# Loading expert 0's second weight in two halves around a value load, with later landings in the schedule

## The chip, the cores and the metric

One core of one Trainium2 chip at a time. The metric is the device time of one execution in microseconds (us). Every kernel gave the reference's result.

## The reference, cut to what matters

Block-sparse attention over 4 batches of 8 heads (768 positions, 64 wide) makes a matrix x of 3072 rows and 512 columns. A mixture of 8 experts follows, with gates from Sinkhorn iterations, so every expert sees every row:

```python
logits = x @ w_gate
P = np.exp(logits - logits.max())
for _ in range(8):
    P /= P.sum(1, keepdims=True) + 1e-09
    P /= P.sum(0, keepdims=True) + 1e-09
    P *= N / E
for e in range(E):                      # E = 8
    h = np.maximum(x @ w1[e], 0.0)      # w1[e]: 512 x 1024
    out += P[:, e:e + 1] * (h @ w2[e])  # w2[e]: 1024 x 512
```

Expert 0 needs no gate until its end, so the kernel runs it beside the attention. Its second weight, w2, is the load that the change is about.

## The kernel before

The kernel describes its work as units, each with an engine, an estimated cost and the units it depends on. A planner puts the units of each engine in order from these estimates alone, and then the program is written in that order. At run time each engine goes through its list in order and waits by semaphores. So an estimate never makes a wait wrong, but it decides what stands ahead of the wait.

```python
def load_w2(e):
    w2s[e] = wpool.tile([128, KF, DM], F16, tag="w2", name="w2")
    nc.gpsimd.dma_start(out=w2s[e][:], in_=moe_w2[e].rearrange("(fk p) d -> p fk d", p=128))

# A load as the planner sees it: issue on POOL, time on the DMA queue,
# and 0.9 us until the data counts as landed.
def load(key, fn, issue, us, deps=()):
    last[0] = add("POOL", issue, fn, [last[0], *deps])
    last[1] = add("DMA", us, None, [add("RING", 0, None, [last[0]], lag=1.4 if last[1] else 0.9), last[1]], 100.0)
    U[key] = add("LAND", 0, None, [last[1]], lag=0.9)

# The projection of expert 0, in two parts: hidden chunks 0-3, then 4-7.
p0 = add("PE", 0.88, lambda c=c: project0(key, c, 0), evac[0:4] + [U["w2"]], pr + 0.1 + c * 0.02, opens=[buf])
p1 = add("PE", 0.88, lambda c=c: project0(key, c, 1), evac[4:8] + [p0], pr + 0.11 + c * 0.02, uses=[buf])

# The order of the loads (cut): the first batch, w1 in four parts, then
load_pair(PB, "kqv")                     # k, q, v of the second batch's first pair of heads
load("w2", lambda: load_w2(0), 0.85, 4.0)
# ... then constants (memsets on POOL) and the later pairs
```

All these loads cast f32 to a 16-bit type and go through one queue, issued by POOL. "Pair" below is a pair of heads; PB = 4 pairs make a batch.

The softmax here doesn't subtract the row's maximum and nothing guards it: scores larger than these inputs give would overflow.

## Time and profile before

| | before |
|---|---|
| median of the first 3 runs | 668.64 us (668.12 to 669.35) |
| profiled span | 666.7 us |
| TensorE (PE) busy | 657.9 us, 99% |
| idle of PE before the first projection with w2 | 1.34 us |

POOL's own timeline (start, length, engine, line, operation, output from input): it shows when the two loads of the argument were issued.

```profile
23.24 1.04 POOL L287 DMA_DIRECT2D vx<-in_v_dram  x1
24.24 0.91 POOL L196 DMA_DIRECT2D w<-in_moe_w_dram  x1
```

An issue is busy for about 1 us, but that is not the landing. In the same trace's list of DMA issues this w2 landed 10.5 us after its issue began, at 34.7.

### The profile page before, as it was taken

The page shows a single profiled execution, that of the slowest core. Times are in us where ns is not written, and L with a number is a line of the kernel's source. Part 1 is how long each engine was busy: PE and PEld are TensorE (multiplying, and loading weights), DVE is VectorE, ACT ScalarE, POOL GpSimd, SP SyncE. Part 2 cuts the span into 40 slices and gives each one's busy share as a digit, 9 for nine tenths or more (in the row PEclk, how much of TensorE's full clock was granted, in tenths as well). Part 3 has the DMA queues.
Part 4 walks back from the last instruction along what each step waited for, and adds up shares of the span by engine and source line. Part 5 has one row for each costly group of instructions (what it writes and reads, how often), then busy time and mean ns, then how long its engine had stood idle before and what let it go on. Part 6 is the DMA issues. An engine that isn't in the chain of part 4 may idle for free.

```text
span 666.7 us, 13260 instructions
## 1 busy us (share of the span) xinstructions
PE 657.9 (99%) x5132; PEld 434.0 (65%) x5132; DVE 549.2 (82%) x1035; ACT 410.5 (62%) x768; POOL 198.3 (30%) x256
## 2 busy tenths in 40 slices
PE   8999999999999999999999999999999999999996
PEld 4656665555676666666666666666666666666665
DVE  7889978799989787888789887888778877988776
ACT  6767766555986566556565665656665656556652
POOL 8899622100132222222221222222122213222123
PEclk9999999999999999999999999999999999999999
DMA  9999992700863647473654656373837465334656
GB/s 168 165 149 145 132 88 43 127 0 1 137 112 64 117 75 116 79 127 64 98 102 76 123 83 106 65 127 61 130 64 130 77 95 95 64 64 112 159 134 198
DMA packets 112542, 67.89 MB, mean 102 GB/s; under 512 B 77920, under 2 KB 90464, under 8 KB 112480
## 3 DMA queue, kind: packets, MB, share of 16 engines
q0 software_dynamic: 94800, 57.46, 65.7%
q1 hardware_dynamic: 17152, 9.58, 6.5%
q8 instruction: 40, 0.66, 0.4%
q14 instruction: 22, 0.18, 0.1%
q10 hardware_dynamic: 528, 0.02, 0.0%
HBM read 52.45 MB, written 6.29 MB: 88 GB/s over the span
## 4 chain that ended last, share of the span: by engine, by line
PE 94%; DMA 3%; POOL 2%; issue 0%; DVE 0%; ACT 0%; POOLq 0%; DVEq 0%
PE yps L813 22%; PE pA L762 22%; PE pY L813 17%; PE pQ L762 11%; PE yps L214 6%; PE hps L209 6%; PE pR L762 5%; DMA w<-in_moe_w_dram 3%; PE sg L345 1%; PE tkq L301 1%; PE av L433 1%; PE vs L355 1%; PE av L439 1%; POOL vx L287 1%; PE tx L548 1%; PE ss L459 1%
## 5 line engine op out<-in xcount | busy, mean ns | idle before, releaser
L813 PEld LDWEIGHTS <-h 128*128 128x128 f16 x2352 | 230.1, 98 | 89.3 <-issue 1.0
L841 POOL DMA_DIRECT2D out_acc<-y x120 | 101.5, 880 | 372.0 <-ACT y L837 97.8
L837 ACT ACTIVATE y<-pY,P_sb 128x256 f32<-128x256 f32 x168 | 79.8, 476 | 124.2 <-PE pY L813 122.5
L828 DVE SCALAR_TENSOR_TENSOR out_acc<-yps,P_sb,out_acc 128x512 f32<-128x512 f32 x128 | 95.2, 744 | 30.2 <-PE yps L813 30.0
L796 DVE TENSOR_TENSOR h<-h 128x1024 f16<-128x1024 f16 x168 | 109.0, 684 | 1.2
L813 PE MATMUL pY<-w,h 128*128 128x256 f16 x672 | 100.2, 273 | 0.6 <-ACT y L837 0.6
L762 PE MATMUL pA<-xT,w 128*128 128x512 f16 x336 | 98.5, 379 | 0.0
L813 PE MATMUL yps<-w2sum,h 128*128 128x256 f16 x672 | 98.1, 273 | 0.0
L813 PE MATMUL yps<-w,h 128*128 128x256 f16 x672 | 93.3, 273 | 0.0
L828 DVE SCALAR_TENSOR_TENSOR out_acc<-pY,P_sb,out_acc 128x512 f32<-128x512 f32 x84 | 62.9, 748 | 29.9 <-PE pY L813 28.2
L762 PEld LDWEIGHTS <-w 128*128 128x128 f16 x672 | 65.8, 98 | 30.9 <-issue 0.2
L762 PEld LDWEIGHTS <-w1sum 128*128 128x128 f16 x504 | 49.3, 98 | 44.2
L784 DVE CUSTOM_DVE_ANT_0 h<-pQ,snap 128x512 f16<-128x512 f32 x84 | 57.6, 685 | 6.0 <-ACT snap L205 3.3
L784 DVE CUSTOM_DVE_ANT_0 h<-pA,snap 128x512 f16<-128x512 f32 x84 | 57.3, 683 | 6.0 <-PE pA L762 5.9
L200 ACT ACTIVATE h<-pA 128x512 f16<-128x512 f32 x84 | 50.6, 603 | 12.4 <-PE pA L762 12.2
L200 ACT ACTIVATE h<-pR 128x512 f16<-128x512 f32 x84 | 50.1, 596 | 7.5 <-PE pR L762 7.4
L205 ACT COPY pR<-pA 128x512 f32<-128x512 f32 x84 | 48.0, 571 | 7.4 <-PE pA L762 6.4
L813 PE MATMUL pY<-w2sum,h 128*128 128x256 f16 x336 | 50.4, 273 | 0.0
L762 PE MATMUL pA<-xsum,w 128*128 128x512 f16 x168 | 50.0, 379 | 0.0
L762 PE MATMUL pQ<-xsum,w1sum 128*128 128x512 f16 x168 | 50.0, 379 | 0.0
L762 PE MATMUL pQ<-xT,w1sum 128*128 128x512 f16 x168 | 50.0, 379 | 0.0
L762 PE MATMUL pA<-xsum,w1sum 128*128 128x512 f16 x168 | 50.0, 379 | 0.0
(149 smaller groups left out, 845.9 us busy)
## 6 DMA issues: line engine op xcount, KB each, us to landing
out_acc<-y POOLq DMA_DIRECT2D x120, 256.0 KB, 3.4
w<-in_moe_w_dram POOLq DMA_DIRECT2D x15, 1024.0 KB, 10.6
out_dram<-out_acc SPq DMA_DIRECT2D x24, 256.0 KB, 2.5
qst<-in_q_dram POOLq DMA_DIRECT2D x32, 96.0 KB, 5.8
vx<-in_v_dram POOLq DMA_DIRECT2D x15, 192.0 KB, 6.6
kst<-in_k_dram POOLq DMA_DIRECT2D x24, 96.0 KB, 6.0
w<-in_moe_w_dram POOLq DMA_DIRECT2D x4, 256.0 KB, 7.9
kst<-in_k_dram POOLq DMA_DIRECT2D x3, 192.0 KB, 4.7
```

The lines of the kernel that those rows point to most:

```text
L200: nc.scalar.activation(out=out, in_=in_, func=AF.Relu, bias=0.0, scale=1.0)
L205: (nc.scalar.copy if eng == "ACT" else nc.vector.tensor_copy)(out=out, in_=in_)
L209: nc.tensor.matmul(hp[:, 0:n], lhsT=w1s[e][:, dk, f * 128:(f + 1) * 128], rhs=xT[:, dk, t0:t0 + n], start=(dk == 0), stop=(dk == KD - 1))
L214: nc.tensor.matmul(yp[:, d], lhsT=h[:, f, c * 128:(c + 1) * 128], rhs=w2s[e][:, f, d], start=(f == 0), stop=(f == KF - 1))
L287: nc.gpsimd.dma_start(out=v_x[i % NQ][:].rearrange("p j g x -> p (j g) x")[:, :, 0:D], in_=v[b, h0:h0 + 2].rearrange("j (g p) d -> p (j g) ...
L762: nc.tensor.matmul(dst[:], lhsT=lhsT, rhs=rhs, start=first and k == 0, stop=k == HK - 1, skip_group_check=True)
L784: nc.vector._custom_dve(dve_ops.TENSOR_ADD_SAT, out=ring(e, p, q)[:, q % 2, blk, :], in0=at[src, e, p, q][:], in1=at.pop(("snap", n, e, p, ...
L796: nc.vector.tensor_tensor(out=h[:, :, out_, :], in0=h[:, :, a, :], in1=h[:, :, b, :], op=op)
L813: nc.tensor.matmul(dst[:, d], lhsT=lhsT, rhs=rhs, start=f == 0 and n in (1, 5, 2), stop=f == HF - 1, skip_group_check=True)
L828: nc.vector.scalar_tensor_tensor(out=o, in0=y, scalar=scalar, in1=o, op0=ALU.mult, op1=ALU.add)
L837: nc.scalar.activation(out=at[key][:, d], in_=src, func=AF.Copy, bias=0.0, scale=P_sb[:, t, e:e + 1])
L841: nc.gpsimd.dma_start(out=o, in_=at.pop(("y", e, p, c, key))[:], accum_op=ALU.add)
```

## The change

The intent is to have the projection's first part wait for half of w2 only, to let that half come ahead of v, and to tell the planner that later loads land later, so that it puts more work ahead of their first use. Cut to its core:

```diff
-    def load_w2(e):
+    def load_w2(e, part=0, parts=1):
...
+        fk = slice(part * KF // parts, (part + 1) * KF // parts)
+        nc.gpsimd.dma_start(out=w2s[e][:, fk, :], in_=moe_w2[e].rearrange("(fk p) d -> p fk d", p=128)[:, fk, :])
...
-        def load(key, fn, issue, us, deps=()):
+        def load(key, fn, issue, us, deps=(), lag=0.9):
...
-            U[key] = add("LAND", 0, None, [last[1]], lag=0.9)
+            U[key] = add("LAND", 0, None, [last[1]], lag=lag)
...          # v of later batches: lag 2.3; their k and q: lag 1.8; first batch: 0.9 as before
-                p0 = add("PE", 0.88, lambda c=c: project0(key, c, 0), evac[0:4] + [U["w2"]],
+                p0 = add("PE", 0.88, lambda c=c: project0(key, c, 0), evac[0:4] + [w2_0[0]],
...
-                p1 = add("PE", 0.88, lambda c=c: project0(key, c, 1), evac[4:8] + [p0],
+                p1 = add("PE", 0.88, lambda c=c: project0(key, c, 1), evac[4:8] + [p0, w2_0[1]],
...
-        load_pair(PB, "kqv")
-        load("w2", lambda: load_w2(0), 0.85, 4.0)
+        load_pair(PB, "kq")
+        load(("w2", 0), lambda: load_w2(0, 0, 2), 0.85, 2.0, (), 2.3)
+        load_pair(PB, "v")
+        load(("w2", 1), lambda: load_w2(0, 1, 2), 0.85, 2.0, (), 2.3)
```

More of the change, by code (lines that the diff above doesn't have):

```diff
@@ L192, in load_w1 @@
             in_=moe_w1[e].rearrange("(dk p) f -> p dk f", p=128)[:, :, part * fw:(part + 1) * fw])
-    def load_w2(e):
-        w2s[e] = wpool.tile([128, KF, DM], F16, tag="w2", name="w2")
-        nc.gpsimd.dma_start(out=w2s[e][:], in_=moe_w2[e].rearrange("(fk p) d -> p fk d", p=128))
+    def load_w2(e, part=0, parts=1):
+        if part == 0:
+            w2s[e] = wpool.tile([128, KF, DM], F16, tag="w2", name="w2")
+        fk = slice(part * KF // parts, (part + 1) * KF // parts)
+        nc.gpsimd.dma_start(out=w2s[e][:, fk, :], in_=moe_w2[e].rearrange("(fk p) d -> p fk d", p=128)[:, fk, :])
     def relu(eng, out, in_):
@@ L869, in load_pair @@
                     load(("v", i), lambda: load_v(i), 1.05, 1.85 if i < PB else 1.6,
-                         [U.get(("A", old, 1)), U.get(("near", old))])
+                         [U.get(("A", old, 1)), U.get(("near", old))], 0.9 if i < PB else 2.3)
                 elif i < PB and c in "qr":
@@ L876, in load_pair @@
                     load((c, i), lambda z=z: load_qk(i, z), 0.75 if i < PB else 1.65,
-                         1.2 if i < PB else 1.4, [U.get(("tr", old, z)), U.get(("tr", old, 2))])
+                         1.2 if i < PB else 1.4, [U.get(("tr", old, z)), U.get(("tr", old, 2))], 0.9 if i < PB else 1.8)
         def pair_start(i, prio):
@@ L991, in expert0 @@
             pr = 1000.0 + n
-            w = [U["w1", n] for n in range(4)]
+            w, w2_0 = [U["w1", n] for n in range(4)], [U["w2", n] for n in range(2)]
             evac, old = [], [U.get(("pj", halves[n - 2], c)) for c in range(HG)] if n >= 2 else []
```

## The prediction

> **What bounds the kernel now.** I read the page's busy lines first, then the PE line of the 40 slices, then the chain of waits, and last the timeline of PE and of POOL around the one DMA piece that stands in that chain late. The page:
>
> ```profile
> PE 657.9 (99%) x5132; PEld 434.0 (65%) x5132; DVE 549.2 (82%) x1035; ACT 410.5 (62%) x768; POOL 198.3 (30%) x256
> PE   8999999999999999999999999999999999999996
> PEclk9999999999999999999999999999999999999999
> ```
>
> TensorE is busy 657.9 of 666.7 us, at the full granted clock in every slice. So only what shortens PE's stream of matmuls, or fills a hole in it, can shorten the kernel: 666.7 - 657.9 = 8.8 us of holes are all there is. The chain of waits says where one of them comes from (start, length, what):
>
> ```profile
> 8.48 2.03 POOL vx L287 x2
> 10.51 0.67 POOL w L190
> 11.18 9.34 DMA w<-in_moe_w_dram
> 20.52 0.28 issue
> 20.81 0.82 POOL kst L282
> 21.63 1.64 POOL qst L282 x2
> 23.27 0.97 POOL vx L287
> 24.24 10.49 DMA w<-in_moe_w_dram
> 34.73 0.04 issue
> 34.77 1.02 PE yps L214 x4
> ```
>
> The last DMA piece is expert 0's w2: issued at 24.24, landed at 34.73. From 34.77 on the chain is PE alone. The timeline of PE at that place:
>
> ```profile
> 31.52 0.81 PE L209 MATMUL hps<-xT,w 128*128 128x384 f16 x4
> 32.26 0.38 PE L345 MATMUL sg<-qT,kT 64*128 64x160 bf16 x6
> 32.58 0.51 PE L548 MATMUL tx<-ident_x,xs 128*128 128x128 f16 x6
> 32.92 0.51 PE L355 MATMUL vs<-vx,m_blk 128*128 128x128 bf16 x6
> 34.77 1.02 PE L214 MATMUL yps<-w,h 128*128 128x512 f16 x4 [1.34 <-DMA w<-in_moe_w_dram]
> ```
>
> PE stands still for 1.34 us until w2 is there. It is the only such hole after the start. The others, from the same timeline: 1.27 before the first matmul, 0.47 + 0.26 + 0.17 for the first q, the first v and a part of w1, before the change has any effect. The stretch 600 to 667 us has 61.59 busy of 67.00, so about 5.1 us lie at the end (66.7 - 61.59): the last results leaving. The rows from 35 to 600 show full slices (100.00 busy in each 100 us). 1.27 + 0.47 + 0.26 + 0.17 + 1.34 + 5.1 = 8.6 of the 8.8.
>
> **What the Trainium skill says.** (1) "Perfetto Trace Analysis", Identifying the Most-Contended Engine: matmul busy share is not a good measure of the distance to roofline, weight-load busy is a better one. Here 99% against 65%, so PE is not at its peak; but this change makes no matmul cheaper, and for a hole in an in-order stream the idle column is what counts. (2) Same page, DMA Instruction - SWDGE: the profiler's end of a GpSimd DMA is the end of descriptor generation, not of the movement. The trace agrees: w2's instruction took 0.91 us, its data landed 10.49 us after it began. So a second half costs POOL about 0.9 us more, and says nothing yet of landing. (3) "DMA: Bandwidth & Descriptors", SWDGE vs HWDGE vs iDMA: only GpSimd DMAs can cast. The weights are cast from f32 to f16, which fits their all being on POOL's queue; there the order of issue decides. (4) Same page, Anatomy of one DMA: about 2.0 us + bytes / 436 GB/s, so 4.4 us for w2's 1 MB. The trace disagrees for this queue: 10.49 us, because w2 stands behind v and others. I use the trace's landings.
>
> **The change, part by part.** *Landings before* (issue plus time to landing, of these single DMAs): the last q of the second batch's first pair lands at 22.43 + 4.5 = 26.9, its v at 23.24 + 5.8 = 29.0, w2 at 34.7. So v took 2.1 us of the queue and w2 5.7.
>
> *The new order* is k, q, first half of w2, v, second half. Estimates from these: first half at 26.9 + 2.85 = 29.8, v at 31.9, second half at 34.7. The bytes ahead of the second half's end are the same, so it does not land sooner than all of w2 does now. What changes is that half of the projection needs only the first half, and that the scheduler knows of later landings (2.3 us for w2 and later v, 1.8 for later k and q, in place of 0.9) and puts other work ahead.
>
> *The instruction order on PE* (compared from the built programs) has 10242 rows (weight loads and matmuls) in both and is identical up to the k transposes at 28.12 us. From there I walk the new order with the distances between starts in the old timeline: k transposes 0.33, hidden x4 0.65, values with summaries 0.84, scores x8 0.32, summaries 0.16, q transposes 0.34, hidden x4 0.65, tx x3 0.17; this is 3.46, so the first projection (first half of w2) stands at 31.6, with 29.8 its landing: 1.8 us to spare. Then yps x4 0.86, values twice 1.68, scores x6 0.32, and vs of that v at 34.4, against 31.9: 2.5 us to spare. Then 0.35 for vs, and the first matmul that needs the second half is at 28.12 + 6.67 = 34.8, against 34.7. So the hole of 1.34 us closes, with nothing to spare at its end. **Removed: 1.34 us.**
>
> *What it adds on POOL.* One more weight DMA, 0.91 us, ahead of the memsets and of all later loads. The next k issue moves from 29.21 to about 30.1. POOL has no more free time between 29 and 72 us (its rows follow one another), but loads wait in the DMA queue anyhow: a q issued at 36.07 took 5.8 us from issue to landing, the first pair's q 4.5. I take 0 to 0.8 us of the shift as reaching the landings, 0.3 as likely.
>
> *Who would feel that.* Old landings: q of the second pair at 31.65 + 6.1 = 37.8, its v at 32.46 + 6.9 = 39.3. New PE order on from 34.8: yps x4 0.86, tx x6 0.34, scores 0.32, yps x4 0.86, ss 0.29, k transposes 0.34; the q transposes stand at 37.8. Again nothing to spare. vs of the second pair follows q transposes 0.34, yps 0.86, logits 0.62 and scores 0.32 later, at 39.9: 0.6 to spare. If q lands 0.3 us later, PE stops 0.3. A stall at the second half of w2 would move this point too, so the two do not add up. **Added: about 0.3 us, 0 to 0.9.** From the third pair on the slack is larger: k lands at 34.28 + 6.2 = 40.5 and is wanted at 42.2.
>
> *What stays.* The order of the engines is the same again from expert 1's second block of tokens on; by then the Sinkhorn iterations (last one at 165.4 us) and the first eight scalings are reordered, but PE had no hole there before and has the same filler (expert 0's last halves). DVE and ACT have the same work. The tail of 5 us is unchanged.
>
> *Sum:* 668.64 - 1.34 + 0.3 = **667.6 us**.
>
> **Rivals.** *A: the wait only moves.* The second half lands late (its 512 rows split over the same engines, one more completion, near-value loads of v now fall into its tail since v lands 2.9 us later), PE stops at 34.8 for it. For it: no spare time in my walk. Against: total bytes are the same, and the PE work put ahead is real. To lose all 1.34 us it would have to land at 36.1. It would give 668.0 to 668.6. *B: the new order hits POOL.* All loads of the second batch land 0.8 us later and PE stops at the second pair's q and v: 668.1 or so. For it: POOL is solidly busy from 29 to 72. Against: the loads queue behind one another in the DMA engines. *C: the better lags remove more than the hole.* There are no other holes to remove after 35 us; a handoff between groups costs about 0.1 us at the same places in both. It would give at most 667.2. *D: the reorder opens a hole far behind,* at a PSUM buffer or at the last gates, of a us or more: 668.6 and more. Before, ACT and DVE had 7.00 and 9.60 of 10 us busy at 50 to 60, so DVE is close; the plan put DVE at its work in another order. I give this 10%.
>
> **Range and chances.** All paths lie within 2% (13.4 us): removing every hole would give only 1.3%. The three runs before spread 668.12 to 669.35, so a median moves by some 0.3. From 1.34 gained in full with a little luck (666.9) to nearly all lost (668.5) holds 8 in 10. Faster by over 2% 0.005, slower by over 2% 0.005.
>
> **What would show it.** In the changed kernel: two w loads of 512 KB in the DMA issues; the row "yps" with no or under 0.4 us idle before it at 31.6, and the second one likewise near 34.8; v landing near 31.9 and the second half near 34.7; PE's idle total down by about 1 us, from 8.8 to 7.8; PE busy unchanged within 0.5 us. Wrong would be: a hole of over 1 us at the second half (rival A), holes before the q transposes or vs at 37 to 41 us (B), any new hole after 45 us (D), or a gain over 1.6 us (then something I hold fixed, such as PE's busy time, has moved).

## The result, and the profile after

| | before | after |
|---|---|---|
| median of 6 runs each | 668.38 us (666.76 to 669.35) | 667.51 us (667.27 to 667.76) |
| ratio | 1 | 0.9989, 95% interval 0.9976 to 1.0003 |
| profiled span | 666.7 us | 665.9 us |
| PE busy | 657.9 us | 658.1 us |

A ratio here is the mean time of one kernel's runs over the mean of the other's runs of the same rounds, so it is not quite the ratio of the medians. The interval includes 1.

The page after, first the busy line and PE's 40 slices, then the row of the DMA issues (how many, kilobytes each, median us from issue to landing) that answers to w2:

```profile
PE 658.1 (99%) x5132; PEld 434.5 (65%) x5132; DVE 550.3 (83%) x1034; ACT 411.8 (62%) x769; POOL 199.0 (30%) x257
PE   8999999999999999999999999999999999999997
...
w<-in_moe_w_dram POOLq DMA_DIRECT2D x2, 512.0 KB, 8.5
```

PE does the same work. There is one POOL instruction more, and two loads of 512 KB stand where one of 1024 KB was. PE's timeline in the changed kernel, at the places that the prediction walked to:

```profile
31.35 1.03 PE L216 MATMUL yps<-w,h 128*128 128x512 f16 x4
...
34.11 0.52 PE L357 MATMUL vs<-vx,m_blk 128*128 128x128 bf16 x6
34.46 1.02 PE L216 MATMUL yps<-w,h 128*128 128x512 f16 x4
...
37.67 0.50 PE L303 MATMUL tkq<-ident,qst 128*128 128x128 bf16 x6
...
39.86 0.52 PE L357 MATMUL vs<-vx,m_blk 128*128 128x128 bf16 x6
```

No row carries an idle time in brackets: the hole of 1.34 us before "yps" is gone, and none has opened at the four later places. POOL's timeline shows the new order of the queue:

```profile
21.32 0.78 POOL L198 DMA_DIRECT2D w<-in_moe_w_dram  x1
22.07 1.05 POOL L289 DMA_DIRECT2D vx<-in_v_dram  x1
23.08 0.80 POOL L198 DMA_DIRECT2D w<-in_moe_w_dram  x1
```

They landed 7.4, 8.7 and 9.6 us after issue, that is at 28.7, 30.8 and 32.7. One thing is not explained by the change: v was issued 1.2 us *earlier* than before (22.07 against 23.24), although it now has a load ahead of it. The whole queue ran earlier in this execution: between 14 and 21 us, ahead of anything changed, POOL waited 4.07 us in all for earlier loads to land in the kernel before, and 2.13 us in the changed one.

Also, the hole was 1.34 us, but the span fell by only 0.8. PE's last row, before and after, shows where the 0.8 lies:

```profile
661.12 1.04 PE L813 MATMUL yps<-w,h 128*128 128x256 f16 x8
660.68 1.04 PE L815 MATMUL yps<-w,h 128*128 128x256 f16 x8
```

PE ended 0.44 us earlier, at 661.72 against 662.16. Of that, 0.25 is the earlier start of the stretch (27.87 against 28.12), so only 0.19 of the 1.34 stayed between the changed place and PE's end: something came back. The rest of the 0.8 lies after PE's end, where the span goes on for 4.5 us in the kernel before and 4.2 us in the changed one. That is not w2's doing. In the four traces with as many POOL loads as the kernel before (its copy, `lags_only` and `w2_ahead` below are the others) it is about 4.5 us; in the ten with one or two more it is about 4.2 us, also where w2 is whole and the plan is old (`before_late`, `w2_later`). So about 0.3 us come with an added POOL load (229 DMAs of POOL against 230 or 231), whichever load it is; why is not shown.

### The profile page after: what moved, and what is told of

It is laid out like the page before. It is cut to its first block, busy times and chain, and to the rows that moved or that the text cites. A ratio compares the mean times of both kernels' runs of the same rounds, so it can differ in the third digit from the quotient of the medians.

```text
span 665.9 us, 13246 instructions
## 1 busy us (share of the span) xinstructions
PE 658.1 (99%) x5132; PEld 434.5 (65%) x5132; DVE 550.3 (83%) x1034; ACT 411.8 (62%) x769; POOL 199.0 (30%) x257
## 4 chain that ended last, share of the span: by engine, by line
PE 93%; DMA 3%; issue 1%; DVE 1%; POOL 0%; ACT 0%; POOLq 0%; DVEq 0%; ACTq 0%
PE yps L815 21%; PE pA L764 21%; PE pY L815 16%; PE pQ L764 10%; PE hps L211 6%; PE yps L216 6%; PE pR L764 5%; DMA out_acc<-y 2%; PE sg L347 1%; PE tkq L303 1%; DMA qst<-in_q_dram 1%; PE vs L357 1%; PE av L435 1%; PE av L512 1%; PE tx L550 1%
## 5 line engine op out<-in xcount | busy, mean ns | idle before, releaser
L764 PE MATMUL pR<-xT,w 128*128 128x512 f16 x168 | 50.0, 379 | 0.0
```

The lines of the kernel that those rows point to most:

```text
L764: nc.tensor.matmul(dst[:], lhsT=lhsT, rhs=rhs, start=first and k == 0, stop=k == HK - 1, skip_group_check=True)
```

## The experiments

### The two theories

*Theory 1 (the loads):* the hole is the whole story. Closing it is worth what the hole was worth, and the extra issue on POOL gives a little back.

*Theory 2 (the plan):* the order of the loads gives the gain, and the planner's new order of instructions costs part of it.

To compare traces without the noise of the start, I use one length throughout, called the **body**: from the start of the first k transposes of the second batch on PE (28.12 in the kernel before; up to there PE's order is the same in all kernels) to the end of the last matmul. Before: last row 661.12 + 1.04 - 28.12 = 634.04 us.

### Each side of the change alone, and the noise (one call, 5 rounds)

The kernel `queue_only` loads the halves in the new order but tells the planner nothing. A comparison of the built programs showed PE, DVE, ACT and SP with exactly the instruction order of the kernel before, and POOL with that of the kernel after.

```diff
-    load(("v", i), lambda: load_v(i), ...)
+    load(("v", i), lambda: (load_w2(0, 0, 2) if i == PB else None, load_v(i)), ...)
-    load("w2", lambda: load_w2(0), 0.85, 4.0)
+    load("w2", lambda: load_w2(0, 1, 2), 0.85, 4.0)
```

> The kernel before with only the order of the loads changed: first half of w2, v, second half; every compute engine keeps the old kernel's instruction order. Theory Q (the new place of w2 in the queue is what closes the hole): the first projection waits only for the first half, 0.0 to 0.2 us idle before it in place of 1.34; the second half is wanted about 2.6 us after that and is there; time as the changed kernel or up to 0.6 us less, ratio to before 0.997 to 1.000. Rival L (the scheduler's later landings do it, by putting other work ahead of the projection): the hole stays above 0.7 us and the time stays within 0.3 us of before.

`lags_only` is the reverse: w2 in one load after v as before, and only the landings of the diff (2.3 for w2 and later v, 1.8 for later k and q).

```diff
-    load("w2", lambda: load_w2(0), 0.85, 4.0)
+    load("w2", lambda: load_w2(0), 0.85, 4.0, (), 2.3)
     # and the lags of v, k and q as in the change
```

> The kernel before with only the scheduler's landing times made later (2.3 us for w2 and v, 1.8 us for k and q of the later batches); w2 is one load behind v as before. By the spacings of the old trace its first projection stands at about 34.4 us. Theory Q: with w2 landing at 34.7 a hole of 0.2 to 0.5 us stays, time 0.5 to 1 us under before. Rival L: the hole is under 0.2 us and the time equals the changed kernel's within 0.3 us. If w2 lands 2 us sooner here, as run to run it may, neither shows a hole.

Two unchanged copies measured the noise:

> A copy of the kernel before, to see another profile of it. Theory V (the landing of w2, and so the hole, changes from run to run, which makes the old kernel's spread of 2.6 us and the changed kernel's narrow 0.5 us): w2 lands at another time than 34.73 by 0.3 us or more, the hole is 1.34 us shifted by the same amount (0 at least), and the span follows. Rival: hole 1.3 us again, w2 at 34.7 within 0.2.

> A copy of the changed kernel, to see another profile and five more times. Theory V: even where the loads land 1 to 2 us later than in its first profile (second half at 32.7 us), idle before either projection is under 0.3 us; times within 667.0 to 668.0. The two small holes of the first profile, 0.48 us behind an accumulating DMA near 555 us and 0.3 us near 180 us: the first is gone or elsewhere if it is chance, at the same place if it belongs to the new order.

Measured against 11 runs of the kernel before (median 667.69):

| | median (range), 6 runs | ratio, 95% | body in the trace |
|---|---|---|---|
| `queue_only` | 666.75 (666.38 to 668.95) | 0.9992 (0.9971 to 1.0012) | 632.55 |
| `lags_only` | 668.42 (666.77 to 669.06) | 1.0006 (0.9986 to 1.0026) | 632.63 |
| `before_again` | 667.25 (666.71 to 671.38) | 1.0003 (0.9978 to 1.0028) | 636.81 |
| `after_again` | 667.81 (667.27 to 670.22) | 1.0007 (0.9984 to 1.0030) | 633.82 |

No interval excludes 1, so the times alone settle nothing. The traces say more. In `queue_only` PE reaches the two parts of the projection without idle time:

```profile
33.12 1.02 PE L216 MATMUL yps<-w,h 128*128 128x512 f16 x4
...
35.77 1.03 PE L216 MATMUL yps<-w,h 128*128 128x512 f16 x4
```

The halves had landed at 29.0 (21.84 + 7.2) and 32.8 (23.59 + 9.2), so 4.1 and 3.0 us to spare. The old instruction order then needs no new plan to be without a hole. That the halves did it is not shown by this trace alone: the queue ran early here too, and a whole w2 landing at 32.8 would also have been in time. The pair `before_late` and `queue_only_late` below, with the same load added to both, is the better evidence. `queue_only`'s body is 1.49 us shorter than that of the kernel before: the 1.34 of idle time, and 0.15 of getting going again.

The unchanged copy `before_again` taught most. Its profiled execution took 671.38 us, and its trace says why. PE's timeline, with the idle time before the row in brackets:

```profile
36.34 1.07 PE L214 MATMUL yps<-w,h 128*128 128x512 f16 x4 [2.71 <-DMA w<-in_moe_w_dram]
```

The stretches of 1 us around it in the same trace (stretch and its length; then busy time and count of PE, weight loads, DVE, ACT and POOL; then the granted PE clock, the DMA share and GB/s):

```profile
36.00:37.00 1.00, 0.66 (x4) 0.30 (x4) 0.00 (x0) 0.00 (x0) 0.17 (x1) 1.00 2.37 164
37.00:38.00 1.00, 1.00 (x18) 0.79 (x16) 0.00 (x0) 0.00 (x0) 1.00 (x2) 0.59 2.38 148
38.00:39.00 1.00, 1.00 (x15) 0.51 (x10) 0.31 (x2) 0.00 (x0) 0.86 (x2) 0.50 2.34 144
...
40.00:41.00 1.00, 1.00 (x7) 0.51 (x5) 0.61 (x2) 0.51 (x2) 1.00 (x2) 0.70 1.52 97
```

The same w2 load was issued 0.2 us later (24.44) but took 11.9 us to land, and the hole was 2.71 us instead of 1.34. In the stretch after the one in which PE starts again, the granted clock falls to 0.59, then to 0.50, and at 40 to 41 it is still at 0.70, with PE busy all the time. The body was 4.26 us longer than `queue_only`'s 632.55: 2.71 of idle time, and some 1.5 of slower matmuls and getting going again. So the size of the hole is no property of the kernel. It is the landing of w2 minus the end of PE's earlier work, and the landing moves.

The page "TensorE: Matmul & The Clock Gate", Part 1, names an idle window of about 3.4 us for the fall to half clock. The half clock agrees (0.50), but here 2.71 us of idle time were enough, while 1.34 us left the clock at 1.00 (and so did 1.67 us in `w2_ahead`, below). The changed kernel is probably not safe from it: one of its runs took 670.22 us at a mean clock of 0.997, as low as that of the bad execution. It was not profiled, and it lies outside the 667.0 to 668.0 expected.

`lags_only` came out without a hole before w2 in its profile: w2 landed at 32.4 (22.54 + 9.9), and the new plan wanted it at 34.18. With a landing at 34.7, as in the first profile, it would have had one. Its unprofiled runs are no faster than the kernel before, so what later landings are worth by themselves stays open.

### Moving the landing on purpose

If theory 1's mechanism holds, a later w2 must cost the old order dearly, and the new one nothing at first. Three kernels got an extra load of 192 KB into a spare tile ahead of the second batch's first k (3 rounds), together with a kernel that has the halves and their dependencies but all lags at 0.9.

```diff
+def load_spare():
+    nc.gpsimd.dma_start(out=spare[:], in_=v[1, 0:2].rearrange("j (g p) d -> p (j g) d", p=128))
-    load((c, i), lambda z=z: load_qk(i, z), ...)
+    load((c, i), lambda z=z: (load_spare() if (i, z) == (PB, 0) else None, load_qk(i, z)), ...)
```

> The kernel before with one more load, of v's size and shape (192 KB) into a spare tile, ahead of the loads of the second batch's first pair; every compute engine's order is unchanged. By the old traces it takes about 2.1 us of the queue. Theory V (the hole before the first projection is as long as w2 is late, 1:1): w2 lands 1.5 to 2.5 us later and the hole is its landing less 33.4 us, so about 3 us, time 669.5 to 670.5, ratio to before above 1.002. Rival (the wait is for something else, or the queue has room): hole and time as before.

> The changed kernel with the same extra load in front. Its first projection is wanted at about 31.4 us, v at 34.1, the second half at 34.5, the loads landed at 28.7 to 30.0, 30.8 to 32.7, 32.7 to 34.6 without the extra load. With 2 us more: first half 31 to 32, v 33 to 35, second half 35 to 36.5. Theory S (the split buys slack of 0 to 2 us and no more): holes of 0.5 to 2.5 us in all before the two projections, v, or the values that need v's edge rows; time 668 to 669.5, so less than before_late by 1 us or more. Rival (the split makes the kernel indifferent to late loads): time within 0.4 us of the changed kernel's 667.5.

> The old order of the engines with the new order of the loads, and the same extra load in front. v is wanted at about 32.9 us, the first half at 33.2, the second half at about 36. With 2 us more than in its profile: first half 31, v 32.5 to 33, second half 35. Theory S: this order has its slack where the landings are, holes under 1 us in all, time 666.5 to 668 and under after_late. Rival: it is as slow as after_late, or the old order needs its v early and stops there for more than 1 us.

This miss is worth telling. The medians were 667.57 (`before_late`, ratio 1.0009), 667.81 (`after_late`, 1.0011) and 667.73 (`queue_only_late`, 1.0002), 4 runs each against 7 of the kernel before (median 667.14), with every interval across 1. PE's timeline in `before_late`:

```profile
34.15 1.02 PE L214 MATMUL yps<-w,h 128*128 128x512 f16 x4 [0.97 <-DMA w<-in_moe_w_dram]
```

And in `queue_only_late`:

```profile
39.72 0.40 PE L445 MATMUL av<-Ve,Ee 128*128 128x130 bf16 x3 [0.63 <-DMA Ve<-vx]
```

With an extra load ahead of it, w2 landed at 34.1 in `before_late`, *earlier* than in the two unchanged profiles (34.7 and 36.3). The dose of about 1 us is smaller than the run-to-run movement, so the times could not decide. The traces of the pair say something: with the same load ahead, the whole w2 cost `before_late` 0.97 us, while in `queue_only_late`, with the same order on PE, the second half landed at 33.6 and neither part of the projection waited. (`after_late` lost 1.08 us at 18.32 to a v of the first batch, ahead of anything changed, and had no hole at the halves.) `queue_only_late` shows something else: a copy that cuts the near rows out of v waited for v, 0.63 us. That is a new wait that comes from v standing behind half of w2. `after_again` has it too, 0.47 us at 41.88.

> The change without its later landings: w2 in two halves around v, the scheduler told of both, but all landing times at the old 0.9 us. If the later landings in the plan are needed, there are holes of over 0.5 us in the stretch 30 to 45 us (the plan wants loads sooner than they are there), and the time is above the changed kernel's by as much. If only the place in the queue counts, it is within 0.5 us of queue_only (666.8).

```profile
38.19 0.49 PE L303 MATMUL tkq<-ident,qst 128*128 128x128 bf16 x6 [0.31 <-DMA qst<-in_q_dram]
39.59 0.51 PE L357 MATMUL vs<-vx,m_blk 128*128 128x128 bf16 x6 [0.91 <-DMA vx<-in_v_dram]
```

In `halves_no_lag` (667.71, ratio 1.0, 0.9984 to 1.0017) the hole at w2 is gone, but two holes stand before q and v of the second pair, together 1.22 us. The second belongs to the plan: v landed at 39.6, 0.2 us later than in the kernel before, but this plan wants it about 10.4 us after the start of the body (28.02), and the plan of the kernel after wants it after 12.0, which would be at 40.0. The first does not: both plans want q 9.8 to 9.9 us after that start, and q landed 0.2 us too late for either in this execution. So with the halves in the plan, the later landings earn their place before v; none of the four profiles of the kernel after (it, its two copies and `after_late`) has idle time at either.

### A larger dose, and the copies again (one call)

`w2_later` puts two spare loads (192 and 128 KB) between v and w2. `w2_ahead` issues the whole of w2 ahead of v. PE's order is that of the kernel before in both.

```diff
-    load("w2", lambda: load_w2(0), 0.85, 4.0)
+    load("w2", lambda: (load_spare(0), load_spare(1), load_w2(0)), 0.85, 4.0)   # w2_later
```

```diff
-    load(("v", i), lambda: load_v(i), ...)
+    load(("v", i), lambda: load_w2(0) if i == PB else load_v(i), ...)           # w2_ahead
-    load("w2", lambda: load_w2(0), 0.85, 4.0)
+    load("w2", lambda: load_v(PB), 0.85, 4.0)
```

> The kernel before with two more loads (of v's kind, 192 and 128 KB, into spare tiles) between the first pair's v and w2; every compute engine's order is unchanged. A dose larger than what the landings differ by from run to run. Theory V (the hole is w2's landing less the end of PE's earlier work, 33.0 to 33.6 us, one for one): w2 lands at 36 to 40, hole of 3 to 6 us, time 669.7 to 673. Rival (PE's wait is not set by w2 alone, or later work absorbs it): time under 669.

> The old order of the engines, w2 whole and ahead of v: w2 lands at about 32 to 34, v last at 34 to 36, wanted at 32.9. If the split is needed: no hole before the projection, but one of 1 to 2.5 us before the summaries of v, so time as before or up to 1 us more. If only w2's being early counts: no hole over 0.3 us, time as queue_only.

`w2_later` was slower beyond the noise: 670.07 (668.43 to 670.91), ratio 1.0030 (1.0009 to 1.0051). Its PE timeline:

```profile
36.18 1.65 PE L214 MATMUL yps<-w,h 128*128 128x512 f16 x4 [2.99 <-DMA w<-in_moe_w_dram]
```

And one stretch after the hole, with the columns as above:

```profile
37.00:38.00 1.00, 1.00 (x8) 0.51 (x6) 0.00 (x0) 0.00 (x0) 1.00 (x2) 0.50 2.44 150
```

w2 landed at 36.1, the hole was 2.99 us, the clock fell to 0.50 again, and the body was 637.14, 4.59 us over `queue_only`'s. That is the bad execution of `before_again` made on purpose, and it shows the cause: with the old order, the time follows w2's landing.

`w2_ahead` was slower too: 669.57, ratio 1.0029 (1.0007 to 1.0051). PE's timeline:

```profile
38.97 0.35 PE L433 MATMUL av<-vx,em 128*128 128x65 bf16 x6
40.98 0.40 PE L439 MATMUL av<-Ve,Ee 128*128 128x130 bf16 x3 [1.67 <-DMA Ve<-vx]
```

The hole did not vanish, it moved: with a whole w2 ahead of it, v landed at 32.9 (22.37 + 10.5), the copy of its near rows came later still, and PE stood 1.67 us for that copy. So what helps is not w2 before v but half of it on either side.

The best candidate and the changed kernel once more, 5 rounds:

> queue_only once more, beside the changed kernel on one chip. Theory O (the new engine order itself costs about 0.6 us that no load explains): lowest time 666.3 to 666.5, mean 0.4 to 0.9 us under the changed kernel's; no hole over 0.2 us before the projections unless the loads come 2 us late. Rival (the earlier difference was chance): mean within 0.3 us of the changed kernel's.

> The changed kernel once more, beside queue_only on one chip. Theory O: lowest time 667.2 to 667.4 again, which no run of the changed kernel has gone under so far, with the hole of 0.3 us near 180 us; mean 667.5 to 668. Rival: lowest time under 666.9.

`queue_only_b`: 666.50 (666.47 to 666.91), ratio 0.9981 (0.9966 to 0.9996). `after_b`: 667.99 (667.29 to 668.58), ratio 1.0 (0.9984 to 1.0015). The kernel before had median 667.43 in 11 runs. So the reordered queue with the *old* plan is the fastest of the three, and the changed kernel is level with the one before. The two means, 666.59 and 667.86, lie 1.27 us apart, more than the 0.4 to 0.9 expected.

### What the new plan costs

The bodies side by side, with the idle time of PE that the trace shows in them:

| trace | plan | idle at known places | body |
|---|---|---|---|
| `queue_only`, `queue_only_b` | old | none | 632.55, 632.67 |
| before | old | 1.34 at w2 | 634.04 |
| `before_again`, `w2_later` | old | 2.71, 2.99 at w2 | 636.81, 637.14 |
| `lags_only` | late landings only | none | 632.63 |
| `after_late` | new | none in its body | 633.20 |
| `after_b` | new | 0.23 at 555.06, at the same matmuls as in the last row | 633.44 |
| `after_again` | new | 0.47 at the copy of v | 633.82 |
| after | new | 0.48 at 554.97, waiting for ACT | 633.85 |

With no accident in it, the new plan's body is 633.20, which is 0.65 us more than `queue_only`'s 632.55. The matmuls are the same. Less their known idle times, all bodies agree with this: 632.55 to 632.77 with the old order on PE and no fallen clock (632.99 in `w2_ahead`), 632.63 in `lags_only`, 633.20 to 633.37 with the halves in the plan, `halves_no_lag` included. About 0.3 of it has an address. The chain of waits of the kernel after, near 180 us (start, length, what):

```profile
179.00 0.45 PE pY L815 x4
179.46 0.02 issue
179.48 0.48 ACT y L839
179.96 0.04 issue
180.00 1.04 PE pY L815 x8
```

The chain goes from PE to ACT and back to PE: PE's next product waits until ACT has read the last one out. In PE's timeline the group around it takes 1.32 us where eight such matmuls in the kernel before take 1.04. This loss of 0.28 us is in each of the four profiles of the new plan (at 179.6, 180.2, 180.1 and 180.8) and in `halves_no_lag`; it is in no profile with the old plan, nor in `lags_only`. So it comes with the halves being known to the planner, not with the later landings. The other 0.3 or so is spread over hand-offs between groups, mostly from 60 to 80 us; I found no single row for it.

All runs together: the kernel before has mean 667.79 (41 runs, 666.66 to 671.38), the kernel after 667.81 (18 runs, 667.27 to 670.22), `queue_only` 666.84 (12 runs, 666.38 to 668.95). The change gains nothing in the mean; its queue alone gains about 0.95 (0.68 first, 1.17 last). About 0.3 of that is the shorter end after PE's last matmul, so 0.6 or so is left for the hole. The standard deviation was 1.16 before and 0.70 after. The fastest run tells the plan's price again: 667.27 after against 666.66 before, although the changed kernel has the shorter end.

Before's fastest runs, 0.3 us from the fastest of `queue_only`, were probably executions in which w2 landed in time: the 0.3 is then the longer end. None of them was profiled, so that is argued and not shown.

## Why the prediction was right or wrong

**What bounds the kernel**, one hole of 1.34 us in PE's stream, was right for that trace. PE's total idle time after is 665.9 - 658.1 = 7.8 us, as foretold. The time, 667.51, lies in the range and 0.1 from the 667.6. One of the other holes was misread: of the 5.1 us "at the end", 0.56 is PE waiting for ACT at 660.69, ahead of its last 12 matmuls. It is there in both kernels, so nothing rests on it.

**The walk along PE** held: 31.35, 34.11, 34.46, 37.67 and 39.86 against the predicted 31.6, 34.4, 34.8, 37.8 and 39.9, with no idle time at any of them. At the first three, most of the difference is the earlier start of the stretch, 27.87 against 28.12.

**The landings** were predicted at 29.8, 31.9 and 34.7, and came at 28.7, 30.8 and 32.7. The queue had started earlier in that execution; in `after_again` the second half landed at 34.6 (24.58 + 10.0), as predicted. The "nothing to spare" of the walk was thus real, but not in each execution.

**"Removed: 1.34 us"** is the term that was mis-sized. It took one execution's hole for the kernel's. The unchanged kernel showed 1.34 and 2.71, the latter with a fallen clock behind it. Over all runs, the reordered queue was worth about 0.95 us (before against `queue_only`), of which the hole is some 0.6 and the shorter end 0.3.

**"Added: about 0.3 us, 0 to 0.9"** had the right size and the wrong cause. It was to come from POOL's extra issue pushing q and v of the second pair. The issues of the halves took 0.78 and 0.80, as estimated, but no profile of the kernel after has a hole there; the planner had been told of later landings, and `halves_no_lag` (0.91 before v) shows what they avoid. What was added instead is the price of the new order, 0.65 us in the bodies.

**"What stays"** failed in its reason: "PE had no hole there before and has the same filler". With the new order it has one, 0.28 us near 180. Rival D (a hole far behind) was true in kind, but of 0.28 us where I had written of a us or more. Rival C's sentence that a hand-off costs the same "at the same places in both" failed with it. "The tail of 5 us is unchanged" failed too: the added load went with an end that is 0.3 us shorter.

**Rival A** (the wait only moves) did not happen with the halves. A wait that only moves is what happened in `w2_ahead`, though there it moved to the copy of v's near rows. **Rival B** did not happen with the later landings. Without them PE stopped at the places that it names, but before v because the plan wanted v sooner: v landed 0.2 us later than in the kernel before, and PE stopped 0.91.

**The sum** came out at 667.6 from 1.34 and 0.3, and matched the first six runs. That closeness was luck: it started from a median of 668.64, 0.85 above the mean of all 41 runs. With what the runs showed, some 0.6 off for the hole, 0.3 off at the end and 0.65 or more on, the gain is near nil, and the pooled means (667.79 and 667.81) say so. The first comparison's gain of 0.7 us (means 668.20 and 667.50) was within its own interval of nothing. What stays open is the rest of the difference of 0.97 between the pooled means of after and `queue_only`: 0.65 is in the bodies; the remainder may be chance waits that differ from run to run, which is not shown.

## What to carry to other kernels

A hole that ends with a load's landing has no fixed size: profile the unchanged kernel twice before taking its length as the gain, because here it was 1.34 us once and 2.71 us plus a fallen clock the next time. When a scheduler orders the program, a change of its inputs is two changes, the one meant and the reordering of all that follows; try the first without the second, as here the new order of the loads under the old plan was the faster kernel (666.50 against 667.99). Look also at the end of the program: here 0.3 us of a gain of 0.95 came after the last matmul and had nothing to do with the wait under study. Splitting a large load around a small one helped where swapping them only moved the wait.

## What the Trainium skill lacked or had wrong

- "TensorE: Matmul & The Clock Gate", Part 1, and its rule in "HAM oscillation" that no idle gap of PE exceed about 3.4 us: here idle times of 2.71 and 2.99 us were already followed by a granted clock of 0.50 and some 1.5 us of loss (in both traces the stretches of 1 us from 36 to 41 fall short of the full clock by 1.71 us in all, as much as 3.4 us at half clock); 1.34 and 1.67 us were not. A limit for safe gaps would have to lie below 2.71 us.
- "DMA: Bandwidth & Descriptors", Anatomy of one DMA: 2.0 us + bytes / 436 GB/s gives, as an estimate, 4.4 us for the 1 MB that w2 takes in its tile (or 6.8 us if the 2 MB of f32 that it reads are meant: the page does not say how a cast counts). Behind other casting loads on one queue it took 9.8 to 11.9 us in six traces. The page gives the time of a load alone, and nothing for one in a full queue.
- No page relates the end of a program to the number of POOL loads: the time after PE's last matmul was about 4.5 us in four traces, 4.2 us in ten.
- No page says how far a landing moves from run to run. The same w2 load of the unchanged kernel landed at 34.7 and 36.3 us in two executions, and the kernel's time moved with it.
